# Chunk attention and a two-layer product: values and row sums of a head from one product, and VectorE's weight sums at other steps

## The chip, the cores and the metric

The kernel runs on one core of a Trainium2 chip. The metric is the device time of one execution in microseconds (us). The kernel before was run 13 times: the median is 294.53 us, the runs lie between 293.27 and 295.85 us. One execution is also recorded by the hardware profiler; all profile lines come from that execution.

## What is computed

Attention within chunks of 64 tokens, and then two matrix products with a leaky ReLU between them. The inputs q, k and v have 8 batches, 8 heads, 576 tokens and 64 dimensions per head, in float32; `w_in` is 512x2048 and `w_out` is 2048x512.

```python
# per batch, head and chunk of 64 tokens:
scores = q_c @ k_c.T / 8
attn = exp(scores - max);  attn /= attn.sum(-1) + 1e-09
x = (attn @ v_c)  ->  [4608 tokens, 512]
h = x @ w_in
g = maximum(0.01 * h, h)
out = g @ w_out
```

## The kernel before

**Blocks.** The 4608 tokens are worked on in 9 blocks (`j`) of 512 tokens, that is 8 chunks. A block has four head pairs (`kk`); the two heads of a pair lie on partitions 0 to 63 and 64 to 127. The products of block `j` run together with the attention of block `j+1`.

**Attention** of a block and head pair has four parts, called at the steps that the lists `steps` give:

- `attn_t` (t) transposes q and k (on TensorE for the first three blocks, by DMA from block 3 on) and copies the two heads of k into `kd`, a matrix that is zero where the heads would mix. For the very first block one of the two copies is on ScalarE, otherwise both are on VectorE.
- `attn_s` (s) makes the scores of both heads with eight products of 64 columns, and ScalarE takes the exponential into `e`.
- `attn_x` (x) makes the row sums `zp` with one product of 512 columns against `onesd` (ones within a head, zero across), and the values `xp` with eight products of 64 columns against `VD`. `VD` holds v for one head and zeros, set once by `clear_vd`, for the other. ScalarE then takes `Ln` of the sums and `Exp` of its negative: the reciprocals `rz`.
- `attn_n` (n) multiplies `xp` by `rz` on VectorE into `xT`, the input of the first product.

**Products.** In step n = 0 to 15 of a block, `mm1` makes one 128-row slice of h from four products of 512 columns, and ScalarE turns it into `gT` with the leaky ReLU. In steps 16 to 31, block 0 makes the second product plainly (`mm2`, four parts of w_out by four slices of tokens). Blocks 1 to 8 make it with seven products instead of eight (M1 to M7, after Strassen), in two halves `u` of seven steps each: `mm2s`, 14 steps of eight products of 256 columns. It needs sums of quarters of w_out (`w_sums`, and `w_in_place`, which overwrites two quarters) and sums of quarters of g (`g_sums`), all on VectorE. ScalarE copies M3 and M4 out of PSUM, and VectorE combines the rest.

**Order and buffers.** The order on each engine is the order in which the program is written (`manual_schedule`): nothing reorders it, and each engine takes its instructions one after the other. Within a step the product comes first, then the attention parts of that step in the order n, x, s, t, then the sums and casts. PSUM has eight banks: four for attention (tag "at") and four for the products ("mm"). A tile takes the bank that has been free longest, and a product that writes a bank waits for the reader of the tile that was there. `rz` has two buffers. SP issues loads and stores, GpSimd the loads that change the type; GpSimd also casts keys and, for the first blocks, queries.

Of the kernel before, what the change touches and what calls it, by code (L numbers as in the profile page):

```python
# [9 lines left out]
FP32 = mybir.dt.float32  # L10
ALU = mybir.AluOpType
AFT = mybir.ActivationFunctionType
# [3 lines left out]
def kernel(  # L16
# [9 lines left out]
    nc = tc.nc  # L26
# [5 lines left out]
    CH = 64  # L32
    NKK = H // 2
    NFC = d_ff // 128
    TB = 512
    NJ = n_tok // TB
    NC = TB // CH
    R = 4
    NI = CH // R
    NPT = 3  # L40
# [10 lines left out]
    onesd = sb.tile([128, 128], FP16, name="onesd")  # L51
# [9 lines left out]
    NVD = 2  # L61
    KD = [sb.tile([128, NC, 2, CH], FP16, name=f"kd{m}") for m in range(NKD)]
    VD = [sb.tile([128, NKK, NC, 2, CH], FP16, name=f"vd{m}") for m in range(NVD)]
# [1 line left out]
        nc.vector.memset(t[0:64, :, 1, :], 0.0)  # L65
        nc.vector.memset(t[64:128, :, 0, :], 0.0)

    def clear_vd(m, eng):
        eng.memset(VD[m][0:64, :, :, 1, :], 0.0)
        eng.memset(VD[m][64:128, :, :, 0, :], 0.0)  # L70

    clear_vd(0, nc.vector)

    w_in = sb.tile([128, NKK, d_ff], FP16, name="w_in")
    w_out = sb.tile([128, NFC, d_model], FP16, name="w_out")
# [20 lines left out]
    def sbuf(shape, dtype, name, bufs):  # L96
        return sb.tile(shape, dtype, name=name, tag=name, bufs=bufs)

    def psum(shape, dtype, name, tag):
        return ps.tile(shape, dtype, name=name, tag=tag, bufs=4)  # L100
# [74 lines left out]

    def attn_t(j, kk):

        if j < NPT:  # L180
            tp = psum([128, 2, R, 128], FP16, "tp", "at")
            tk = psum([128, 2, R, 128], FP16, "tk", "mm") if j == 0 else tp
            for a, t in enumerate((tp, tk)):
                for r in range(R):
                    nc.tensor.transpose(
                        out=t[:, a, r, :], in_=half[j][a][:, kk, r, :, :], identity=ident
                    )
            qt = sbuf([128, R, 128], FP16, "qt", 2)
            nc.vector.tensor_copy(out=qt, in_=tp[:, 0, :, :])
            kt = tk[:, 1, :, :]  # L190
        else:
            qt, kt = (t[:, kk, :, :] for t in trans[j])
        kd = KD[(j * NKK + kk) % NKD]
        for hh in range(2):
            p0 = hh * 64
            dst = kd[p0:p0 + 64, :, hh, :].rearrange("p c (i r) -> p c i r", r=R)
            src = kt[p0:p0 + 64, :, :].rearrange("p r (c i) -> p c i r", i=NI)
            if j == 0 and kk < 3 and hh == 0:
                nc.scalar.activation(out=dst, in_=src, func=AFT.Copy, bias=0.0, scale=1.0)
            else:  # L200
                nc.vector.tensor_copy(out=dst, in_=src)  # L201
        live[j, kk] = (qt, kd)
# [16 lines left out]

    def attn_x(j, kk):  # L220

        e = live[j, kk]
        zp = psum([128, TB], FP32, "zp", "at")
        nc.tensor.matmul(out=zp, lhsT=onesd, rhs=e, start=True, stop=True)  # L224
        xp = psum([128, R, 128], FP32, "xp", "at")
        for c in range(NC):
            nc.tensor.matmul(  # L227
                out=xp[:, :, c * NI:(c + 1) * NI],
                lhsT=VD[j % NVD][:, kk, c, :, :],
                rhs=e[:, :, c * NI:(c + 1) * NI],  # L230
                start=True,
                stop=True,
            )
        rz = sbuf([128, TB], FP32, "rz", 2)
        nc.scalar.activation(out=rz, in_=zp, func=AFT.Ln, bias=0.0, scale=1.0)  # L235
        nc.scalar.activation(out=rz, in_=rz, func=AFT.Exp, bias=0.0, scale=-1.0)  # L236
        live[j, kk] = (xp, rz)

    def attn_n(j, kk):

        if j not in xT:
            xT[j] = sbuf([128, NKK, TB], FP16, "xT", 2)
        xp, rz = live.pop((j, kk))
        nc.vector.tensor_tensor(  # L244
            out=xT[j][:, kk, :], in0=xp.rearrange("p r t -> p (r t)"), in1=rz, op=ALU.mult
        )

    STEPS = (attn_t, attn_s, attn_x, attn_n)

# [43 lines left out]
    wv = w_out.rearrange("p (i e) (h m) -> p e h i m", e=2, h=2)  # L293
    ws = {n: sb.tile([128, NH, MH], FP16, name=f"ws_{n}") for n in ("b11_22", "b11_12", "b21_11")}
    gs: dict[str, bass.AP] = {}

    def tt(eng, out, in0, in1, op):
        eng.tensor_tensor(out=out, in0=in0, in1=in1, op=op)  # L298

    def w_sums(g, eng):  # L300

        i = slice(2 * g, 2 * g + 2)
        b11, b12, b21, b22 = (wv[:, e, h, i, :] for e in range(2) for h in range(2))
        tt(eng, ws["b11_22"][:, i, :], b11, b22, ALU.add)
        tt(eng, ws["b11_12"][:, i, :], b11, b12, ALU.add)
        tt(eng, ws["b21_11"][:, i, :], b21, b11, ALU.subtract)

    def w_in_place(g, eng):

        i = slice(2 * g, 2 * g + 2)  # L310
        tt(eng, wv[:, 0, 1, i, :], wv[:, 0, 1, i, :], wv[:, 1, 1, i, :], ALU.subtract)
        tt(eng, wv[:, 1, 0, i, :], wv[:, 1, 0, i, :], wv[:, 1, 1, i, :], ALU.add)

    def g_quarters(j):
        gv = gT[j].rearrange("p (i e) (h t) -> p h e i t", e=2, h=2)
        return [gv[:, h, e, :, :] for h in range(2) for e in range(2)]

    def g_sums(j, g):

        if g == 0:  # L320
            for n in ("a11_12", "a21_22", "a11_22"):
                gs[n] = sbuf([128, NH, TB // 2], FP16, n, 1)
        i = slice(2 * g, 2 * g + 2)
        a11, a12, a21, a22 = (x[:, i, :] for x in g_quarters(j))
        tt(nc.vector, gs["a11_12"][:, i, :], a11, a12, ALU.add)
        tt(nc.vector, gs["a21_22"][:, i, :], a21, a22, ALU.add)
        tt(nc.vector, gs["a11_22"][:, i, :], a11, a22, ALU.add)
        tt(nc.vector, a21, a21, a11, ALU.subtract)
        tt(nc.vector, a12, a12, a22, ALU.subtract)
# [13 lines left out]
            out=out[j * TB:(j + 1) * TB, :].rearrange("(p r) m -> r p m", r=R)[ti], in_=osb  # L343
        )

    part: dict[str, bass.AP] = {}

    def mm2s(j, u, step):

        a11, a21_11, a12_22, a22 = (g_quarters(j)[n] for n in (0, 2, 1, 3))  # L350
        b11, b12_22, b21_22, b22 = wv[:, 0, 0], wv[:, 0, 1], wv[:, 1, 0], wv[:, 1, 1]
        lo, hi = slice(0, MH), slice(MH, d_model)

        def bank(n):
            part[n] = psum([128, d_model], FP32, "mp", "mm")[:, lo]
# [51 lines left out]
    with tc.manual_schedule():  # L407
# [9 lines left out]
        for step in range(NKK + 2):  # L417
# [10 lines left out]
            p = step - 2  # L428
            if 0 <= p < NKK:
                attn_x(0, p)  # L430
            p = step - 1
# [4 lines left out]
            p = step - 2  # L436
# [7 lines left out]
                mm1_part(0, hp, fc, kk)  # L444
        for fc, hp in enumerate(hps):
            mm1_end(0, hp, fc)
        clear_vd(1, nc.vector)
        alloc(1)
        for kk in range(NKK):
            first = load_qk(1, 2 * kk, 2 * kk + 2)[0]  # L450
# [15 lines left out]

        def regular(first, gap, lags=(0, 3, 5, 7)):
            return [[first + gap * kk + lag for kk in range(NKK)] for lag in lags]

        for j in range(NJ):
# [16 lines left out]
            for n in range(2 * NFC + (16 if j == 0 else 0)):  # L489
                if n >= 2 * NFC:  # L490
                    pass
                elif n >= NFC:
                    if j == 0:
                        mm2(j, *reversed(divmod(n - NFC, 4)))
                    elif n - NFC < 14:
                        mm2s(j, *divmod(n - NFC, 7))
                elif j or n >= len(hps):
                    mm1(j, n)
                if hw_at.get(n, NJ) < NJ:
# [7 lines left out]
                        load_qk(qk_at[n], H // 2, H)  # L507
                        after(first, last, "the first two blocks' operands come first")
                for stage, kk in at.get(n, ()):
                    stage(j + 1, kk)  # L510
                if j and n in (4, 8, 12, 16):
                    g_sums(j, n // 4 - 1)
                if j == 0 and n in (20, 23, 26, 32):
                    w_sums((n - 20) // 3 if n < 32 else 3, nc.vector)
                if j == 1 and n < 4:
                    w_in_place(n, nc.vector)
                if j + 2 < NJ:
                    if n in range(cast_at, cast_at + 8, 2):
                        kk = (n - cast_at) // 2
# [41 lines left out]
```

The softmax here doesn't subtract the row's maximum and nothing guards it: scores larger than these inputs give would overflow.

## Time and profile before

| | us |
|---|---|
| median of 13 runs | 294.53 |
| time of the profiled execution | 294.56 |
| its span, first to last instruction | 292.8 |
| TensorE busy (matmul) | 278.0, 95% |
| VectorE busy | 210.3, 72% |
| ScalarE busy | 159.9, 55% |
| GpSimd busy | 107.4, 37% |

The time is 1.76 us more than the span. The share of an engine is an average over stages: the first block has short waits of all engines on each other, and from block 3 on one engine works without a gap. A start-to-start distance between two instructions of one engine is shorter than the duration that the record of one shows[...].

### The profile page before, as it was taken

Reading aid. Unit: us, or ns where it says so; the run is one execution under the profiler, and the core shown is the slowest. Engines: PE = TensorE matmul, PEld = TensorE weight load, DVE = VectorE, ACT = ScalarE, POOL = GpSimd, SP = SyncE. Lnnn points to the kernel's source line nnn. Section 1 sums busy time; section 2 is a strip of 40 time slices with the busy share of each in tenths; the row PEclk is TensorE's granted clock in tenths of the full one; section 3 lists DMA queues with packets and bytes.
Section 4 is the critical chain, followed back from the end, with each engine's and each line's share of the span. In section 5 each row is a group of like instructions: output and inputs, shape, how many; then the busy total and the mean of one; then the engine's idle time right before and its main releaser. Section 6 shows DMA issues by size and latency. Waiting matters only on the chain.

```text
span 292.8 us, 5954 instructions
## 1 busy us (share of the span) xinstructions
PE 278.0 (95%) x2264; PEld 179.3 (61%) x2264; DVE 210.3 (72%) x462; ACT 159.9 (55%) x288; POOL 107.4 (37%) x165
## 2 busy tenths in 40 slices
PE   6979997999799989999999999999999999999994
PEld 2544544446674468557854785488448844884583
DVE  6371455999974898799789779787778748863554
ACT  2567514467245755586358636853684378436610
POOL 5673755844950391087078009406400000000000
PEclk9999999999999999999999999999999999999999
DMA  8999999999999999999978996996770120021011
GB/s 182 232 161 240 244 200 218 238 227 194 194 121 219 273 111 222 185 224 203 238 198 108 231 195 164 170 304 128 110 143 2 73 75 0 2 92 55 0 72 74
DMA packets 92605, 46.28 MB, mean 158 GB/s; under 512 B 65440, under 2 KB 87968, under 8 KB 92576
## 3 DMA queue, kind: packets, MB, share of 16 engines
q1 hardware_dynamic: 68896, 39.33, 58.6%
q0 software_dynamic: 23680, 6.56, 21.5%
q8 instruction: 18, 0.29, 0.4%
q14 instruction: 11, 0.09, 0.1%
HBM read 36.70 MB, written 9.44 MB: 158 GB/s over the span
## 4 chain that ended last, share of the span: by engine, by line
PE 67%; DVE 3%; issue 0%; ACT 0%
PE mp L333 31%; PE hp L251 31%; PE sp L209 2%; PE xp L227 2%; PE zp L224 2%; DVE kd L201 1%; DVE a L298 1%; DVE qh L156 1%; DVE gT L298 0%; ACT gT L262 0%; DVE osb L298 0%
## 5 line engine op out<-in xcount | busy, mean ns | idle before, releaser
L251 PE MATMUL hp<-xT,w_in 128*128 128x512 f16 x576 | 130.9, 379 | 0.2 <-DVE xT L244 0.2
L262 ACT ACTIVATE gT<-hp 128x512 f16<-128x512 f32 x144 | 84.9, 596 | 48.2 <-PE hp L251 47.8
L251 PEld LDWEIGHTS <-w_in 128*128 128x128 f16 x576 | 54.3, 98 | 60.1 <-DMA w_in<-in_moe_w_in_dram 0.8
L298 DVE TENSOR_TENSOR a<-gT 128x512 f16<-128x512 f16 x96 | 40.1, 472 | 24.8 <-ACT gT L262 24.3
L333 PEld LDWEIGHTS <-gT 128*128 128x128 f16 x512 | 49.8, 98 | 7.4
L156 POOL CAST kh<-kf 128x512 f16<-128x512 f32 x36 | 24.8, 704 | 79.9 <-DMA kf<-in_k_dram 75.1
L137 POOL DMA_DIRECT2D vd<-in_v_dram x64 | 43.5, 697 | 2.5 <-DMA w_out<-in_moe_w_out_dram 2.1
L298 DVE TENSOR_TENSOR osb<-mp,m 128x256 f32<-128x256 f32 x64 | 26.9, 422 | 16.1 <-ACT e L217 8.4
L333 PEld LDWEIGHTS <-a 128*128 128x128 f16 x384 | 35.8, 98 | 3.8
L235 ACT ACTIVATE rz<-zp 128x512 f32<-128x512 f32 x36 | 21.4, 595 | 29.0 <-PE zp L224 27.8
L333 PE MATMUL mp<-ws_b,gT 128*128 128x256 f16 x256 | 33.2, 273 | 0.0
L333 PE MATMUL mp<-w_out,gT 128*128 128x256 f16 x256 | 32.0, 273 | 0.0
L201 DVE COPY kd<-kT 64x512 f16<-64x512 f16 x48 | 30.7, 639 | 0.3
L333 PE MATMUL mp<-w_out,a 128*128 128x256 f16 x256 | 30.9, 273 | 0.0
L244 DVE TENSOR_TENSOR xT<-xp,rz 128x512 f16<-128x512 f32 x36 | 24.6, 685 | 7.2 <-ACT rz L236 5.6
L165 POOL CAST vd<-vf 64x512 f16<-64x512 f32 x36 | 24.6, 684 | 10.0 <-DMA vf<-in_v_dram 8.0
L217 ACT ACTIVATE e<-sp 128x512 f16<-128x512 f32 x36 | 21.3, 592 | 11.3 <-PE sp L209 11.2
L298 DVE TENSOR_TENSOR gT<-gT 128x512 f16<-128x512 f16 x64 | 26.9, 461 | 0.0
L236 ACT ACTIVATE rz<-rz 128x512 f32<-128x512 f32 x36 | 22.7, 630 | 1.1
L209 PEld LDWEIGHTS <-kd 128*128 128x128 f16 x288 | 12.7, 100 | 11.3 <-DVE kd L201 8.3
L227 PEld LDWEIGHTS <-vd 128*128 128x128 f16 x288 | 13.6, 99 | 7.8 <-issue 1.5
L367 ACT ACTIVATE m<-mp 128x256 f32<-128x256 f32 x16 | 6.1, 383 | 21.3 <-PE mp L333 21.3
(44 smaller groups left out, 212.1 us busy)
## 6 DMA issues: line engine op xcount, KB each, us to landing
out_dram<-osb SPq DMA_DIRECT2D x36, 256.0 KB, 3.0
w_in<-in_moe_w_in_dram POOLq DMA_DIRECT2D x4, 512.0 KB, 7.6
w_out<-in_moe_w_out_dram POOLq DMA_DIRECT2D x4, 512.0 KB, 13.0
qf<-in_q_dram SPq DMA_DIRECT2D x4, 384.0 KB, 7.8
kf<-in_k_dram SPq DMA_DIRECT2D x4, 384.0 KB, 11.6
qf<-in_q_dram SPq DMA_DIRECT2D x5, 256.0 KB, 6.7
kf<-in_k_dram SPq DMA_DIRECT2D x5, 256.0 KB, 7.2
qf<-in_q_dram SPq DMA_DIRECT2D x2, 640.0 KB, 9.5
```

The lines of the kernel that those rows point to most:

```text
L137: eng.dma_start(out=dst, in_=v[b, h, s:s + n, :].rearrange("(c p) d -> p c d", p=CH))
L156: eng.tensor_copy(out=half[j][a][:, kk, :, :, :], in_=raw[j][a][:, 2 * kk:2 * kk + 2, :].rearrange("p h (r d) -> p r h d", r=R),)
L165: nc.gpsimd.tensor_copy(out=dst, in_=src)
L201: nc.vector.tensor_copy(out=dst, in_=src)
L217: nc.scalar.activation(out=e, in_=sp, func=AFT.Exp, bias=0.0, scale=SCL)
L235: nc.scalar.activation(out=rz, in_=zp, func=AFT.Ln, bias=0.0, scale=1.0)
L236: nc.scalar.activation(out=rz, in_=rz, func=AFT.Exp, bias=0.0, scale=-1.0)
L244: nc.vector.tensor_tensor(out=xT[j][:, kk, :], in0=xp.rearrange("p r t -> p (r t)"), in1=rz, op=ALU.mult)
L251: nc.tensor.matmul(out=hp, lhsT=w_in[:, kk, fc * 128:(fc + 1) * 128], rhs=xT[j][:, kk, :], start=(kk == 0), stop=(kk == NKK - 1),)
L262: nc.scalar.activation(out=gT[j][:, fc, :], in_=hp, func=AFT.Prelu, bias=0.0, scale=1.0, alpha=0.01)
L298: eng.tensor_tensor(out=out, in0=in0, in1=in1, op=op)
L333: nc.tensor.matmul(out=o, lhsT=a[:, i, u * 128:(u + 1) * 128], rhs=b[:, i, :], start=(i == 0), stop=(i == NH - 1),)
```

## The change

Five things are changed together.

1. `VD` holds ones, not zeros, beside v (`ones_vd` in place of `clear_vd`). In `attn_x` the product against `onesd` is gone. Instead of eight products over all 128 rows there are 16 over 64 rows each, one for each head and chunk, alternating between the two row halves and between two banks `xa` and `xb`. A bank has the values of one head on its own 64 partitions and that head's row sums on the other 64.
2. `Ln` is therefore two instructions (each from the other half's partitions), and `attn_n` two multiplications, each over 64 partitions and 512 columns.
3. In `attn_t` from block 3 on, when it is called at step 16 or later, ScalarE makes one of the two key copies.
4. `mm2s` goes through its 14 steps in another order: M3 and M4 of both halves first.
5. `w_sums` and `w_in_place` are called at other steps of block 0 (`w_in_place` was in block 1), and `g_sums` takes its first four slices at once at step 8 for blocks above 2, where it was two and two at steps 4 and 8.

```diff
-    def clear_vd(m, eng):
-        eng.memset(VD[m][0:64, :, :, 1, :], 0.0)
-        eng.memset(VD[m][64:128, :, :, 0, :], 0.0)
+    def ones_vd(m, eng):
+        eng.memset(VD[m][0:64, :, :, 1, :], 1.0)
+        eng.memset(VD[m][64:128, :, :, 0, :], 1.0)
...
-            if j == 0 and kk < 3 and hh == 0:
+            if hh == 0 and (j == 0 and kk < 3 or j >= NPT and n >= NFC):
                 nc.scalar.activation(out=dst, in_=src, func=AFT.Copy, bias=0.0, scale=1.0)
...
         e = live[j, kk]
-        zp = psum([128, TB], FP32, "zp", "at")
-        nc.tensor.matmul(out=zp, lhsT=onesd, rhs=e, start=True, stop=True)
-        xp = psum([128, R, 128], FP32, "xp", "at")
+        xs = [psum([128, R, 128], FP32, n, "at") for n in ("xa", "xb")]
         for c in range(NC):
-            nc.tensor.matmul(
-                out=xp[:, :, c * NI:(c + 1) * NI],
-                lhsT=VD[j % NVD][:, kk, c, :, :],
-                rhs=e[:, :, c * NI:(c + 1) * NI],
-                start=True,
-                stop=True,
-            )
+            for hh, x in enumerate(xs):
+                rows = slice(hh * CH, (hh + 1) * CH)
+                nc.tensor.matmul(
+                    out=x[:, :, c * NI:(c + 1) * NI],
+                    lhsT=VD[j % NVD][rows, kk, c, :, :],
+                    rhs=e[rows, :, c * NI:(c + 1) * NI],
+                    start=True,
+                    stop=True,
+                )
         rz = sbuf([128, TB], FP32, "rz", 2)
-        nc.scalar.activation(out=rz, in_=zp, func=AFT.Ln, bias=0.0, scale=1.0)
+        for hh, x in enumerate(xs):
+            nc.scalar.activation(
+                out=rz[hh * CH:(hh + 1) * CH, :],
+                in_=x[(1 - hh) * CH:(2 - hh) * CH, :, :].rearrange("p r t -> p (r t)"),
+                func=AFT.Ln, bias=0.0, scale=1.0,
+            )
...
-        nc.vector.tensor_tensor(
-            out=xT[j][:, kk, :], in0=xp.rearrange("p r t -> p (r t)"), in1=rz, op=ALU.mult
-        )
+        for hh, x in enumerate(xs):
+            rows = slice(hh * CH, (hh + 1) * CH)
+            nc.vector.tensor_tensor(
+                out=xT[j][rows, kk, :],
+                in0=x[rows, :, :].rearrange("p r t -> p (r t)"),
+                in1=rz[rows, :],
+                op=ALU.mult,
+            )
...
+    ORDER = [(0, 0), (0, 1), (1, 0), (1, 1)] + [(u, s) for u in range(2) for s in range(2, 7)]
...
+        W_SUMS, W_IN_PLACE = (20, 24, 27, 30), (21, 25, 32, 33)
...
-                        mm2s(j, *divmod(n - NFC, 7))
+                        mm2s(j, *ORDER[n - NFC])
...
-                if j and n in (4, 8, 12, 16):
-                    g_sums(j, n // 4 - 1)
-                if j == 0 and n in (20, 23, 26, 32):
-                    w_sums((n - 20) // 3 if n < 32 else 3, nc.vector)
-                if j == 1 and n < 4:
-                    w_in_place(n, nc.vector)
+                sums_at = {8: (0, 4)} if j > 2 else {4: (0, 2), 8: (2, 4)}
+                sums_at |= {12: (4, 6), 16: (6, 8)}
+                if j and n in sums_at:
+                    g_sums(j, *sums_at[n])
+                if j == 0 and n in W_SUMS:
+                    w_sums(W_SUMS.index(n))
+                if j == 0 and n in W_IN_PLACE:
+                    w_in_place(W_IN_PLACE.index(n))
```

## The prediction, made before the changed kernel ran

> **What bounds the kernel now.** I read the page's busy shares, the waits of TensorE, the chain that ended last, stretches of one block each, the groups by line, and the timelines of VectorE and ScalarE at three places. First the busy shares and TensorE's waits (us in total, times, longest):
>
> ```profile
> PE 278.0 (95%) x2264; PEld 179.3 (61%) x2264; DVE 210.3 (72%) x462; ACT 159.9 (55%) x288; POOL 107.4 (37%) x165
> ```
>
> ```profile
> PE sp L209 <- DVE kd L201: 4.7, 6, 1.5
> PE op L277 <- DMA w_out<-in_moe_w_out_dram: 1.8, 1, 1.8
> ```
>
> TensorE is the bound, and waits in few places: for key copies, once for weights. TensorE's timeline places them: in the first attention (15.4, 17.9 us), 1.75 us for w_out at 45.44, then for key copies 0.51 at 65.35, 1.54 at 78.01, 0.61 at 82.54 (block 1), 0.91 at 105.05 (block 2). One later block (us; share of each engine, with counts), and a piece of the chain in it:
>
> ```profile
> 205.17:233.94 28.77, 28.77 (x245) 19.48 (x244) 21.74 (x53) 17.40 (x32) 2.82 (x4) 1.00 0.45 83
> ```
>
> ```profile
> 210.58 0.21 PE zp L224
> 210.80 0.23 PE xp L227 x8
> 211.03 4.32 PE hp L251 x20
> ```
>
> Blocks 3 to 7 take 28.77 us each, with TensorE busy in all of it. So x costs 0.446 us of path per head pair (sums 0.215, values 8 products in 0.23, 29 ns each). What VectorE and ScalarE do costs nothing there while it comes in time. The groups that the change multiplies (busy, mean ns):
>
> ```profile
> L201 DVE COPY kd<-kT 64x512 f16<-64x512 f16 x48 | 30.7, 639 | 0.3
> L235 ACT ACTIVATE rz<-zp 128x512 f32<-128x512 f32 x36 | 21.4, 595 | 29.0 <-PE zp L224 27.8
> L244 DVE TENSOR_TENSOR xT<-xp,rz 128x512 f16<-128x512 f32 x36 | 24.6, 685 | 7.2 <-ACT rz L236 5.6
> ```
>
> **What the Trainium skill says.** TensorEngine Tiling (Array Packing), Key Properties: tiles of the array work independently, but changing the tiling mode drains TensorE. TensorE: Matmul & The Clock Gate, Part 3 (packing small matmuls): matmuls in different row groups start some 4 ns apart; its Part 1 states a start-to-start floor of about 25 ns. Nothing in the trace has 64 rows, so none of the three is shown; the 29 ns above fit the floor. VectorE: DVE Perf Modes, Zero memsets can be issued as uint32: a memset takes a cycle per element whatever the type, and only zeros get the half count. The trace agrees with the half: `vd` was cleared as 64x1024 uint32.
>
> **The change part by part.** Baseline is the profiled span, 292.8; the time is 1.76 more (294.56 against the median 294.53).
>
> *The products of x.* The columns streamed are the same: 512 + 8x64 before, 16x64 after. From below: the two halves stream together and the switches cost nothing, 8 x (29 + 4) = 0.26 us. From above: no overlap, 16 x 29 = 0.46, and each of two switches shows the whole latency of a matmul, 193 - 27 = 0.166 (a 64-column record less its columns): 0.79. I take overlap (0.26) and two drains of about half that latency (0.17): 0.43, no change against 0.446. Ends: -0.19 and +0.34 per call, about 32 calls not otherwise hidden.
>
> *Ones for zeros, at the start.* VectorE before:
>
> ```profile
> 3.16 0.91 DVE L69 MEMSET vd<- 64x1024 uint32 x1 [0.25 <-issue]
> 4.32 0.91 DVE L70 MEMSET vd<- 64x1024 uint32 x1 [0.25 <-issue]
> 5.26 0.72 DVE L156 CAST qh<-qf 128x512 f16<-128x512 f32 x1
> ```
>
> The cast starts without a wait: the memsets, not the load, hold the first queries. Start to start a memset is 1.16 us for 1024 elements and 0.36 for 256, so 1.04 ns each; 2048 elements take 2.2, two of them +2.1 us. The first attention is a serial chain, and four more doubled pieces join it: pair 0's second multiplication ahead of pair 3's copies 0.6 (start to start), pair 1's, whose bank pair 3's scores take, 0.6, pair 3's second `Ln` 0.5 and multiplication 0.6. Sum +4.4: the third slice of `mm1`, complete at 21.35 before, comes at 25.7. Of this, 1.75 falls into the wait for w_out, which is a transfer and does not move (loads are not behind the memsets in any queue), and 0.32 into two waits for GpSimd at 42. Left: +2.3. The second pair of memsets (21.5) is followed by 6 us of idle VectorE; without that it would be +2.1.
>
> *End of block 0.* Here four x stand at steps 25 to 28, one product apart (1.3 us). ScalarE per pair: 1.2 us before, 1.7 after; VectorE 0.6, then 1.2. Before:
>
> ```profile
> 47.58 0.60 ACT L235 ACTIVATE rz<-zp 128x512 f32<-128x512 f32 x1 [6.10 <-PE zp L224]
> 48.21 0.63 ACT L236 ACTIVATE rz<-rz 128x512 f32<-128x512 f32 x1
> 48.75 0.58 ACT L217 ACTIVATE e<-sp 128x512 f16<-128x512 f32 x1
> ```
>
> I count from the end of pair 0's x (47.61 before). Now both banks of a pair are held until the multiplication, where `zp` was free after `Ln`. In the changed program pair 1's `xb` takes the bank of pair 3's scores: it waits for `e` (behind Ln, Ln, Exp) to 2.25, where TensorE is there at 1.1. Pair 3's banks are pair 1's: they wait for pair 1's multiplications, which stand on VectorE behind the output copy of step 28 (4.9 to 5.5) and end at 6.75; TensorE is there at 4.9. Then pair 3's x to 7.2, its copies, Ln, Ln, Exp to 9.0; VectorE's queue (copy, pair 2, copy, pair 3) ends at 11.85. Block 1's first slice needs that, and got it at 7.8 before (55.38). Cost +4.1 (ends 2.5 and 5).
>
> *Block 1 and 2.* Half of `w_in_place` (1.8 of 3.58 us) now lies in block 0's idle VectorE, and TensorE comes some 6 us later while GpSimd's casts, which slow VectorE here (sums of 1.1 us take 2.4), are bound to loads and stay. The new wait: `w_in_place` at steps 21 and 25 must let TensorE finish reading that part of w_out. Pair 3's key copies (step 22) stand behind the first; part 0 is read at step 19, so nothing is late, and if it were, the price is the 1.75 us that TensorE waits at 45.44 anyway. `w_sums` at 27 and 30 stand behind multiplications that are later still. M3 and M4 first move four of the six combinations behind pair 3's copies (1.5 us earlier), against 0.6 for a second multiplication. I let the waits of 2.66 go but for 0.3: block 1 -2.2 with 0.16 lost at its end (below); block 2 -0.7 of 0.91.
>
> *Blocks 3 to 7.* VectorE in the middle of a block before:
>
> ```profile
> 212.40 0.69 DVE L244 TENSOR_TENSOR xT<-xp,rz 128x512 f16<-128x512 f32 x1 [0.67 <-ACT rz L236]
> 213.00 1.21 DVE L201 COPY kd<-kT 64x512 f16<-64x512 f16 x2
> 214.24 1.09 DVE L298 TENSOR_TENSOR a<-gT 128x512 f16<-128x512 f16 x3
> ```
>
> From the block's start, `rz` of pair 0 comes at 7.7 (second `Ln`). Then in VectorE's order: two multiplications 1.2, two copies 1.2, the merged sums 5 x 0.6 = 3.0, the next five 1.75, two multiplications 1.2, two copies 1.25: 17.35. The third scores want them at 222.09 - 205.17 = 16.92: +0.45, as the sums moved from step 4 (idle before) to 8. The merging itself saves 5 fixed parts of 0.07. At the end of the block ahead, pair 3's multiplication ran from 204.67 to 205.35; the second ends 0.6 later, at 205.95, and TensorE wants it after three products of the new block, at 205.17 + 0.65 = 205.82: +0.15 with the semaphore. Five blocks x 0.6 = +3.0 (ends 0.8, if the middle one has half a us of slack that I missed, and 6 where GpSimd slows VectorE). The key copy on ScalarE (0.59, six times) and the order of the halves cost and bring nothing here: ScalarE is 17.4 of 28.8 busy, the last copy is not late. Without that cover a copy costs 0.6.
>
> Sum: 0 + 2.3 + 4.1 - 2.2 - 0.7 + 3.0 = +6.5. Span 299.3, time 301.1 (2.2% slower).
>
> **Rivals.** *Row halves overlap fully* (place: every x; price: 0.25 us or less). For: the skill's 4 ns. Against: the drain. It takes 32 x 0.19 = 6.1; with the other terms at their low ends (2.3 + 2.5 - 2.66 - 0.9 + 0.8 = +2.0) the span is 288.7, with the middle ones 293.2: 290.5 to 295, I say 292.5, faster. It decides from 0.38 us per call with the low ends, 0.24 with the middle ones. *Dear switches*: x near 0.75 in every call, +0.3 x 32 = 9.6 less about 2 that falls into the waits: 308.7. For: two latencies are the natural size of a drain. Against: the drain may be of the array only. *Hidden anyway*: the doubled work finds slack, blocks 3 to 7 lose 0.8 and block 0's end 2.5, x is unchanged: 292.8 + 2.3 + 2.5 - 2.9 + 0.8, time 297.3. For: VectorE is 76% busy in such a block. Against: the chain above is in series.
>
> **How the numbers follow.** Forecast 0.43 (own range 298 to 304), full overlap 0.23, hidden 0.19, dear switches 0.15. Leaving a tenth on each side, half of the overlap case below and two thirds of the dear one above, gives 292.5 to 306. A measurement can tell about 0.2% (0.6 us) from no change. Faster is most of the overlap case, 0.21; same 0.06, from its upper end and the lower end of the hidden one; slower 0.73.
>
> **What would show it.** The group of x: 16 products from start to the next line in 0.43 us; gaps around it tell the drains. The first `hp` complete near 25.7, and still no gain by 45. TensorE waiting for `e` and `xT` between steps 26 and 28 of block 0, block 1 about 6 us late. Waits for `kd` at 65 and 82 gone, new ones of 0.45 before the third scores and 0.15 at each block's start. Wrong if x is far from 0.43, or if blocks 3 to 7 keep 28.77 less a gain.

## The result, and the profile after

The changed kernel takes 314.93 us (median of 11 runs, 313.83 to 316.93), the kernel before 294.67 in runs beside it: a ratio of 1.0698, 95% interval 1.0673 to 1.0723. It is 7.0% slower; the prediction said slower by 2.2%, and its range ended at 306.0. The profiled execution has a span of 312.1 us, 19.3 more than before.

The busy shares, and then TensorE's waits (us in total, times, longest):

```profile
PE 280.5 (90%) x2516; PEld 173.9 (56%) x2516; DVE 224.3 (72%) x461; ACT 188.3 (60%) x331; POOL 103.5 (33%) x165
```

```profile
PE sp L209 <- DVE kd L201: 8.4, 15, 0.9
PE hp L262 <- DVE xT L252: 5.9, 9, 1.8
PE tp L185 <- DVE qh L156: 3.4, 1, 3.4
PE xa L228 <- ACT e L217: 2.0, 2, 1.5
```

TensorE fell from 95 to 90% busy. It waits for key copies 15 times where it did 6 times, and for the multiplications (`xT`) at the start of all eight blocks. One later block took 28.77 us before; now (us; busy time of each engine, with counts):

```profile
219.31:250.24 30.93, 29.42 (x274) 18.73 (x272) 23.33 (x51) 20.86 (x37) 1.47 (x3) 1.00 0.42 78
```

TensorE's timeline in that block shows where the 2.17 us lie:

```profile
220.41 2.97 PE L262 MATMUL hp<-xT,w_in 128*128 128x512 f16 x13 [0.29 <-DVE xT L252]
...
230.62 0.41 PE L209 MATMUL sp<-qT,kd 128*128 128x64 f16 x8 [0.52 <-DVE kd L201]
...
232.37 0.38 PE L262 MATMUL hp<-xT,w_in 128*128 128x512 f16 x1
232.68 0.20 PE L228 MATMUL xa<-e,vd 64*128 64x64 f16 x1
232.69 0.20 PE L228 MATMUL xb<-e,vd 64*128 64x64 f16 x1
...
232.90 0.19 PE L228 MATMUL xb<-e,vd 64*128 64x64 f16 x1
233.02 2.76 PE L262 MATMUL hp<-xT,w_in 128*128 128x512 f16 x12
...
238.10 0.41 PE L209 MATMUL sp<-qT,kd 128*128 128x64 f16 x8 [0.57 <-DVE kd L201]
...
245.20 0.39 PE L209 MATMUL sp<-qT,kd 128*128 128x64 f16 x8
```

The figure in brackets counts idle time from the modelled end of the product before; measured against an undisturbed block (second scores 10.18, third 16.92 us after its start), four things are late: the start by 0.45, then the second scores by 0.69 more, the third by 0.73, the fourth by 0.30. Together 2.17. The x between them is cheap. Two row halves start 3 or 4 ns apart in the trace's own nanoseconds (0 or 10 in the rounded lines), a pair of them every 29 or 30 ns. The first starts 0.31 us after the product ahead of it, where two such products are 0.22 apart, and the next product starts 0.12 after the last. From the product ahead to the product behind that makes 0.65 us; with the sums and the Values of before it was 0.66.

Set block by block against before, by the first slice of `mm1` that has all four pairs (us by which it comes later than before), the shift is as follows (where that slice doesn't wait, as in most blocks before, it is taken 0.65 us, three products, after the block's start):

| reached | later by | term of the stage | predicted |
|---|---|---|---|
| end of pair 0's x, step 25 of block 0 | 2.6 | start 2.6 | 2.3 |
| block 1's first slice (63.26 against 55.38) | 7.9 | end of block 0: 5.3 | 4.1 |
| block 2's | 7.1 | block 1: -0.8 | -2.2 |
| block 3's | 7.7 | block 2: +0.6 | -0.7 |
| block 8's | 19.1 | blocks 3 to 7: +11.4 | +3.0 |
| end of the span | 19.3 | last block: +0.2 | 0 |

The 11.4 us are five times 2.17 and 0.50 more before the fourth scores of block 4. The ScalarE and VectorE groups that were doubled (busy us, mean ns):

```profile
L252 DVE TENSOR_TENSOR xT<-xa,rz 64x512 f16<-64x512 f32 x36 | 24.4, 679 | 28.4 <-ACT rz L242 28.0
...
L237 ACT ACTIVATE rz<-xa 64x512 f32<-64x512 f32 x36 | 21.4, 595 | 21.9 <-PE xb L228 21.2
L201 DVE COPY kd<-kT 64x512 f16<-64x512 f16 x41 | 25.6, 625 | 0.7
L252 DVE TENSOR_TENSOR xT<-xb,rz 64x512 f16<-64x512 f32 x36 | 25.0, 695 | 0.8
...
L237 ACT ACTIVATE rz<-xb 64x512 f32<-64x512 f32 x36 | 21.2, 589 | 0.9
```

An instruction on 64 partitions takes what one on 128 took (589 to 595 ns against 595 for the `Ln`, 679 to 695 against 685 for the multiplication). And its neighbours overlap with it less: VectorE in the same block,

```profile
227.90 0.68 DVE L252 TENSOR_TENSOR xT<-xa,rz 64x512 f16<-64x512 f32 x1 [4.51 <-ACT rz L242]
228.61 0.69 DVE L252 TENSOR_TENSOR xT<-xb,rz 64x512 f16<-64x512 f32 x1
229.34 1.22 DVE L201 COPY kd<-kT 64x512 f16<-64x512 f16 x2
230.59 1.90 DVE L309 TENSOR_TENSOR a<-gT 128x1024 f16<-128x1024 f16 x3
...
234.61 0.75 DVE L309 TENSOR_TENSOR gT<-gT 128x512 f16<-128x512 f16 x2
235.40 0.68 DVE L252 TENSOR_TENSOR xT<-xa,rz 64x512 f16<-64x512 f32 x1
236.11 0.69 DVE L252 TENSOR_TENSOR xT<-xb,rz 64x512 f16<-64x512 f32 x1
236.84 1.20 DVE L201 COPY kd<-kT 64x512 f16<-64x512 f16 x2
```

shows 0.71 from one multiplication to the next and 0.73 to the copy, where before it was 0.60 from the one multiplication to the copy: 1.44 for what had taken 0.60. On ScalarE the two `Ln` start 0.62 apart. Between 227.90 and 238 VectorE is never idle: each pair's late multiplications push its copies, the sums, the next multiplications and the next copies.

### The profile page after: what moved, and what is told of

It reads as the page before. It is cut to its first block, busy times and chain, and to the rows that moved or that the text cites. A ratio compares the mean times of both kernels' runs of the same rounds, so it can differ in the third digit from the quotient of the medians.

```text
span 312.1 us, 6496 instructions
## 1 busy us (share of the span) xinstructions
PE 280.5 (90%) x2516; PEld 173.9 (56%) x2516; DVE 224.3 (72%) x461; ACT 188.3 (60%) x331; POOL 103.5 (33%) x165
## 4 chain that ended last, share of the span: by engine, by line
PE 51%; DVE 32%; ACT 8%; issue 6%; POOL 1%; DVEq 0%
PE hp L262 21%; PE mp L344 20%; DVE xT L252 10%; DVE kd L201 7%; DVE a L309 5%; ACT rz L237 5%; DVE gT L309 4%; PE op L288 4%; PE sp L209 2%; PE xa L228 2%; ACT rz L242 2%; DVE osb L309 2%; DVE m L309 2%; PE tp L185 1%; ACT kd L199 1%
## 5 line engine op out<-in xcount | busy, mean ns | idle before, releaser
L262 PE MATMUL hp<-xT,w_in 128*128 128x512 f16 x576 | 132.3, 379 | 5.9 <-DVE xT L252 5.9
L273 ACT ACTIVATE gT<-hp 128x512 f16<-128x512 f32 x144 | 83.0, 595 | 46.8 <-PE hp L262 46.7
L156 POOL CAST kh<-kf 128x512 f16<-128x512 f32 x36 | 22.5, 639 | 86.5 <-DMA kf<-in_k_dram 86.2
L252 DVE TENSOR_TENSOR xT<-xa,rz 64x512 f16<-64x512 f32 x36 | 24.4, 679 | 28.4 <-ACT rz L242 28.0
L309 DVE TENSOR_TENSOR a<-gT 128x512 f16<-128x512 f16 (+1 forms) x78 | 34.6, 499 | 13.8 <-ACT gT L273 13.3
L237 ACT ACTIVATE rz<-xa 64x512 f32<-64x512 f32 x36 | 21.4, 595 | 21.9 <-PE xb L228 21.2
L165 POOL CAST vd<-vf 64x512 f16<-64x512 f32 x36 | 23.6, 656 | 19.3 <-DMA vf<-in_v_dram 11.5
L201 DVE COPY kd<-kT 64x512 f16<-64x512 f16 x41 | 25.6, 625 | 0.7
L252 DVE TENSOR_TENSOR xT<-xb,rz 64x512 f16<-64x512 f32 x36 | 25.0, 695 | 0.8
L309 DVE TENSOR_TENSOR gT<-gT 128x512 f16<-128x512 f16 (+1 forms) x52 | 24.8, 518 | 0.0
L237 ACT ACTIVATE rz<-xb 64x512 f32<-64x512 f32 x36 | 21.2, 589 | 0.9
```

The lines of the kernel that those rows point to most:

```text
L156: eng.tensor_copy(out=half[j][a][:, kk, :, :, :], in_=raw[j][a][:, 2 * kk:2 * kk + 2, :].rearrange("p h (r d) -> p r h d", r=R),)
L165: nc.gpsimd.tensor_copy(out=dst, in_=src)
L237: nc.scalar.activation(out=rz[hh * CH:(hh + 1) * CH, :], in_=x[(1 - hh) * CH:(2 - hh) * CH, :, :].rearrange("p r t -> p (r t)"), func=AFT. ...
L252: nc.vector.tensor_tensor(out=xT[j][rows, kk, :], in0=x[rows, :, :].rearrange("p r t -> p (r t)"), in1=rz[rows, :], op=ALU.mult,)
L262: nc.tensor.matmul(out=hp, lhsT=w_in[:, kk, fc * 128:(fc + 1) * 128], rhs=xT[j][:, kk, :], start=(kk == 0), stop=(kk == NKK - 1),)
L273: nc.scalar.activation(out=gT[j][:, fc, :], in_=hp, func=AFT.Prelu, bias=0.0, scale=1.0, alpha=0.01)
```

## The experiments

Theory 1: x costs TensorE what it did; the loss is lateness from the doubled `Ln` and multiplications. Theory 2: the 64-row products or the switches between tile shapes cost. Theory 3: the reorderings (merged sums, order of the halves, a key copy on ScalarE) make the waits. Ratios are to the kernel before, in runs beside it, with 95% intervals.

### The reorderings without [V | 1]

```diff
-        xs = [psum([128, R, 128], FP32, n, "at") for n in ("xa", "xb")]
...
+        zp = psum([128, TB], FP32, "zp", "at")
+        nc.tensor.matmul(out=zp, lhsT=onesd, rhs=e, start=True, stop=True)
+        xp = psum([128, R, 128], FP32, "xp", "at")
...
-        eng.memset(VD[m][0:64, :, :, 1, :], 1.0)
+        eng.memset(VD[m][0:64, :, :, 1, :], 0.0)
...
```

> The reorderings alone: the changed kernel with the old attention core (sums by zp, values by xp, zeros in vd, one Ln and one multiplication a pair). Theory 1 (the loss comes from the doubled 64-row Ln and multiplications, late on ScalarE and VectorE): blocks 3 to 7 go back to 28.77 us, the end of block 0 to 7.8 us after pair 0's x, and the waits of 2.66 us in blocks 1 and 2 shrink: 292 to 294 us. Theory 2 (the 64-row products or their switches cost): the same here, 292 to 294. Theory 3 (the merged sums, the order of the halves and the key copy on ScalarE make the waits of blocks 3 to 7): those blocks stay near 30.9, 304 to 306 us.

Measured: 293.59 us, ratio 0.9953 (0.9920 to 0.9986), span 290.7. Blocks 1, 2, 3 and a later one:

```profile
53.54:85.75 32.21, 30.89 (x277) 21.18 (x276) 29.91 (x61) 17.50 (x32) 20.90 (x31) 1.00 1.12 196
85.75:115.36 29.61, 28.95 (x247) 19.41 (x244) 22.56 (x51) 19.65 (x34) 12.10 (x18) 1.00 1.07 211
115.36:145.39 30.03, 28.95 (x247) 19.38 (x244) 22.70 (x47) 18.48 (x33) 13.33 (x18) 1.00 1.19 215
202.93:231.70 28.77, 28.77 (x247) 19.46 (x245) 20.50 (x47) 18.38 (x33) 1.58 (x3) 1.00 0.52 83
```

Theory 3 is out as the cause of the loss. Blocks 1 and 2 gain 1.88 and 0.61 (they took 34.09 and 30.22), so the gain predicted for them (2.2 and 0.7) exists where [V | 1] doesn't use it up. Block 3 loses 1.26: TensorE waits 1.08 us for keys there, with merged sums ahead of them.

### [V | 1] without the reorderings

```diff
-        zp = psum([128, TB], FP32, "zp", "at")
...
+        xs = [psum([128, R, 128], FP32, n, "at") for n in ("xa", "xb")]
...
```

> [V | 1] alone, on the kernel before: its own order of products, its own sums, both key copies on VectorE. Theory 1: the start costs 2.6, the end of block 0 5.3; in blocks 3 to 7 the wait at the start (0.45) and before the second scores (0.69) stay, that before the third scores goes as the sums are not merged behind the multiplications, that before the fourth shrinks to between 0 and 0.3: 5.7 to 7.2 over five blocks; sum 308 to 311 us. Theory 2: all of the loss is here, 314 to 316. Theory 3: the start alone, 296 to 298.

Measured: 318.88 us, ratio 1.0852 (1.0791 to 1.0913), more than any of the three forecasts: the whole loss is here, and the reorderings take 4 us of it back. A later block takes 31.1 to 31.6, with waits before the second, third and fourth scores (0.50, 0.48, 0.44 in brackets). That contradicts a detail of theory 1 as I had put it: the wait before the third scores doesn't come from merging the sums, since it is there without.

### One Ln and one multiplication, with all 16 products

```diff
-        for hh, x in enumerate(xs):
-            nc.scalar.activation(
-                out=rz[hh * CH:(hh + 1) * CH, :],
-                in_=x[(1 - hh) * CH:(2 - hh) * CH, :, :].rearrange("p r t -> p (r t)"),
-                func=AFT.Ln, bias=0.0, scale=1.0,
-            )
+        nc.scalar.activation(
+            out=rz, in_=xs[1].rearrange("p r t -> p (r t)"), func=AFT.Ln, bias=1.0, scale=0.0
+        )
...
+            out=xT[j][:, kk, :], in0=xs[0].rearrange("p r t -> p (r t)"), in1=rz, op=ALU.mult
...
```

> The changed kernel with its 16 row-half products, but one Ln and one multiplication of 128 partitions a pair, in place of two of 64 each. Left out: the normalisation (the Ln is of a constant, and Values of the second head and its sums are mixed up). Theory 1: the loss goes but for the start (0.5 to 2.6) and a little at the end of block 0, where both banks of a pair are still held until the multiplication: blocks 3 to 7 back to 28.8, 294 to 297 us. Theory 2: the products are all there, so the loss is too: 312 to 315. Theory 3: blocks 3 to 7 stay near 30.9, 305 to 308.

Measured: 294.27 us, ratio 1.0007 (0.9972 to 1.0041). A later block:

```profile
205.22:233.98 28.76, 28.76 (x274) 19.00 (x272) 20.43 (x47) 18.44 (x33) 1.47 (x3) 1.00 0.45 83
```

The stretch has 274 products, as in the changed kernel, and takes 28.76 us, where before it was 28.77. From block 1's first whole slice to block 3's it is 61.3 us, as with the reorderings alone (61.5), against 63.8 in the changed kernel; from the end of pair 0's x in block 0 to block 1's first whole slice it is 7.8 us, as before. Theory 2 is out: 16 row-half products with their switches cost TensorE what one product for the sums and eight for the Values cost. One remark on the expectation: here the bank of `xb` is free after the `Ln`, since the multiplication reads only `xa`; so of the end of block 0 this run shows less than it said.

### One of the two doubled instructions at a time

The chain theory: a pair's x, two `Ln`, `Exp`, two multiplications, two key copies, next scores must fit into five products' time; the next three runs take pieces out of it. First one `Ln` (the first half of the edit above), with two multiplications:

> The changed kernel with one Ln of 128 partitions and still two multiplications a pair. Left out: the normalisation (the Ln is of a constant). Chain theory: rz comes 0.62 earlier; of a later block's waits 0.69 becomes 0.07, 0.73 becomes 0.11, 0.30 goes, and the 0.45 at the start, where the multiplications follow an output combination and not rz, stays: 5 x 1.54 less, and about 2 at the start and the end of block 0: 305 us. Rival (half of the loss belongs to each doubled instruction, in proportion): 304 to 305 here and in the next run alike.

Measured: 309.78 us, ratio 1.0501 (1.0453 to 1.0549). Then two `Ln` and one multiplication (the second half of that edit):

> The changed kernel with two Ln and one multiplication of 128 partitions a pair. Left out: the second head's Values in xT are replaced by sums. Chain theory: 0.71 less in VectorE's part of the chain: all four waits of a later block shrink to 0.04 or nothing, 5 x 2.1 less, and about 3 at the end of block 0, 1 at the start: 300 us. Rival (in proportion): 304 to 305.

Measured: 296.97 us, ratio 1.0068 (1.0044 to 1.0091). A later block takes 30.20 us with one `Ln`, 28.76 with one multiplication. Neither the chain's figures (305 and 300 us) nor equal shares (304 to 305 in both) were right: one `Ln` brings 0.73 of 2.17 a block, one multiplication all of it. VectorE with one `Ln` shows why:

```profile
224.73 0.68 DVE L249 TENSOR_TENSOR xT<-xa,rz 64x512 f16<-64x512 f32 x1 [3.76 <-ACT rz L239]
...
231.46 0.76 DVE L306 TENSOR_TENSOR gT<-gT 128x512 f16<-128x512 f16 x2
232.25 0.68 DVE L249 TENSOR_TENSOR xT<-xa,rz 64x512 f16<-64x512 f32 x1
232.96 0.69 DVE L249 TENSOR_TENSOR xT<-xb,rz 64x512 f16<-64x512 f32 x1
233.69 1.21 DVE L201 COPY kd<-kT 64x512 f16<-64x512 f16 x2
```

Its multiplications at 232.25 come straight after the sums. `rz` is there early, and VectorE's queue makes the third scores late (by 0.69; with two `Ln` it was 0.73). So the wait before the second scores belongs to the chain through ScalarE and VectorE and goes with either mend; the one before the third belongs to VectorE's queue and goes only with the multiplication. With one multiplication the copies for the third scores end at 223.92, 16.67 us after the block's start, 0.25 before TensorE wants them; with one of each, at 15.94. The slack before the change was about 1 us, one more `Ln` uses up most of it, and whatever comes on top is paid in full.

### Key copies ahead of the multiplications

```diff
-                for s in (3, 2, 1, 0):
+                for s in (0, 3, 2, 1) if j > 2 else (3, 2, 1, 0):
```

> The changed kernel; in blocks 3 to 7 the key copies of a pair stand ahead of the two multiplications of the pair before, instead of behind them (only the order within a step changes). Theory 1, now sharper (the loss of a later block is the length of one chain: x, Ln, Ln, Exp, two multiplications, two copies, next scores, which has five products' time): the copies leave the chain, the waits before the second, third and fourth scores (0.69, 0.73, 0.30) go, that at the block's start (0.45) stays: 5 x 1.72 less, 306 to 307 us. Rival (VectorE has too much work in all, so the waits come back at the sums or the outputs): less than 3 us gained, 312 to 315.

Measured: 306.73 us, ratio 1.0405 (1.0363 to 1.0447); a later block:

```profile
215.29:244.62 29.33, 29.04 (x275) 18.95 (x273) 23.20 (x51) 20.64 (x37) 1.48 (x3) 1.00 0.44 82
```

The same instructions, in another order on VectorE, and 1.6 us of the 2.17 are gone; 0.56 is left, nearly all of it at the block's start. VectorE is not short of time, 23.2 of 29.3 us; what hurt was that copies which need nothing from a pair stood behind that pair's multiplications.

### The start: ones, and the clock

```diff
-        eng.memset(VD[m][0:64, :, :, 1, :], 1.0)
+        eng.memset(VD[m].bitcast(FP32)[0:64, :, :, 1, :], 0.007826805114746094)
...
```

> The changed kernel, its ones written two at a time as 32-bit words, so that each memset has 1024 elements as the zeros before. Theory 1: a memset takes 1.16 us again, the first cast comes 2.1 us earlier, and as the changed program waits for w_out no more, of this between 0.5 and 2.1 us arrives at the end: 312.8 to 314.4. Against it: the start is absorbed by the wait for w_out, which comes back: 314.9.

Measured: 312.81 us, ratio 1.0657 (1.0580 to 1.0735). This interval holds the changed kernel's 1.0698, so the time alone doesn't tell. The span is 0.7 less, though the first transpose came 2.5 us earlier (5.75 against 8.26).

Nothing in the prediction spoke of TensorE's granted clock. The first stretches of the changed kernel (the third figure from the end is the clock) and, last, the first of the kernel before:

```profile
0.00:10.00 10.00, 5.09 (x19) 2.17 (x19) 6.45 (x13) 1.87 (x2) 5.91 (x14) 0.89 1.04 219
10.00:20.00 10.00, 7.09 (x95) 4.09 (x95) 5.91 (x10) 6.27 (x11) 8.65 (x14) 0.84 1.14 186
20.00:30.00 10.00, 6.82 (x65) 3.64 (x65) 6.64 (x9) 6.78 (x12) 3.11 (x5) 0.92 1.18 239
...
0.00:10.00 10.00, 6.90 (x31) 3.02 (x32) 5.32 (x13) 2.47 (x3) 5.27 (x13) 1.00 1.01 208
```

In stretches of 2 us the changed kernel's clock was 0.50 from 8 to 10 and 0.53 from 18 to 20. But the 1.00 of the kernel before is not what its products show. Three idle products of 512 columns, twice in the kernel before (L394) and twice in the changed one (L407):

```profile
6.88 1.49 PE L394 MATMUL warm<-wz,onesd 128*128 128x512 f16 x3
13.56 0.81 PE L394 MATMUL warm<-wz,onesd 128*128 128x512 f16 x3
...
9.09 1.49 PE L407 MATMUL warm<-wz,onesd 128*128 128x512 f16 x3
11.65 0.81 PE L407 MATMUL warm<-wz,onesd 128*128 128x512 f16 x3
```

They take 1.49 us where the changed kernel's clock was 0.50, and 1.49 us in the kernel before as well, until 13.2 us. So both attentions ran about 7 us at half speed: before from 6.1 to 13.2, in the changed kernel twice 3.4. With the reorderings alone, whose first attention is the same as before, the products ran at full speed from 5.8 us on, and `mm1` began 1.7 us earlier (17.73 against 19.41).

The Trainium skill, TensorE: Matmul & The Clock Gate, Part 1, says that the clock is halved after an idle window of about 3.4 us and that the windows run freely. The changed kernel's first fall fits that: TensorE stood still for 3.42 us before 8.26. The second doesn't: from 14 to 18 TensorE was busy for 1.64 of 4 us. So:

```diff
-        keep_warm(8)
+        keep_warm(14)
...
-            if step < NKK:
-                keep_warm(3)
+            keep_warm((3, 3, 6, 6, 6, 0)[step])
```

> The changed kernel with more idle products on TensorE in its first attention (14 instead of 8 ahead, 6 instead of 3 in the later steps), so that the granted clock, which fell to 0.50 at 8 to 11 and 18 to 21 us, stays at 1.00. Theory: transposes, scores and x at half clock lengthen the serial chain of the first attention by 0.5 to 1.5 us: 313.4 to 314.4 us. Against it: the chain there is ScalarE's and VectorE's, and the clock costs nothing: 314.9.

Measured: 313.16 us, ratio 1.0633 (1.0572 to 1.0694), a little less than forecast; this interval, too, overlaps the changed kernel's. From 5 to 30 us the clock is 1.00, and block 0's first output product starts at 38.30 instead of 39.76. Of these 1.46 us 0.38 are there already at the first transposes (7.88 against 8.26), which wait for a cast on VectorE; the other 1.1 go with the clock. At block 1's first slice 0.5 is left in the profile (62.79 against 63.26). The clock fell at the end of block 0 in this execution (0.83 between 50 and 60); whether that took the rest was not tried.

The larger memsets are not on the path for 2.1 us. The second pair's transposes start at 8.80 with the faster ones, at 9.41 with the faster ones and the idle products together (the last run below), and at 10.15 with the idle products alone. So 0.7 to 1.4 of 2.1 us are left there, since GpSimd casts that pair's queries behind a load (TensorE waits 0.61 and 1.01 for it). In the last run the clock fell to 0.50 between 10 and 13 us, and block 0's first output product came at 38.63, no earlier than 38.30.

### x of block 0 spread out

```diff
-                0: [[10, 14, 18, 22], [13, 17, 21, 25], [25, 26, 27, 28], [27, 28, 29, 30]],
+                0: [[10, 14, 18, 22], [13, 17, 21, 25], [18, 22, 26, 28], [20, 24, 28, 30]],
```

> The changed kernel; the four x of block 0 stand at steps 18, 22, 26 and 28 instead of 25 to 28, their multiplications two steps behind. Theory (the end of block 0 lost 5.3 us since four doubled chains and held banks fall into four steps): block 1's first slice comes 3.5 to 5 us earlier, and most of it stays: 310 to 312 us. Rival (VectorE's total work at the end of block 0 is what counts, or the two late waits move into block 1): 314 to 315.

Measured: 311.47 us, ratio 1.0548 (1.0495 to 1.0601). Block 1's first whole slice starts at 59.23 instead of 63.26: 4.0 of the 5.3 us are the crowding of four doubled chains into four steps. In the changed kernel the waits there are

```profile
52.69 0.19 PE L228 MATMUL xb<-e,vd 64*128 64x64 f16 x1 [1.10 <-ACT e L217]
...
56.73 0.19 PE L228 MATMUL xa<-e,vd 64*128 64x64 f16 x1 [1.37 <-DVE xT L252]
...
63.26 6.42 PE L262 MATMUL hp<-xT,w_in 128*128 128x512 f16 x29 [1.77 <-DVE xT L252]
```

for the banks that the prediction named, and for the last multiplication; the first two are gone when spread.

### All mends together, and a faster kernel without [V | 1]

The last three: the reorderings alone with sums merged only from block 4 on (`if j > 3`); the same with the key copies of block 2, and of the third pair in block 1, a step earlier,

```diff
-                1: [[7, 11, 17, 20], [10, 14, 20, 23], [14, 18, 23, 26], [16, 20, 25, 28]],
-                2: regular(9, 4),
+                1: [[7, 11, 16, 20], [10, 14, 20, 23], [14, 18, 23, 26], [16, 20, 25, 28]],
+                2: [[8, 12, 16, 20]] + regular(9, 4)[1:],
```

and the changed kernel with the mends of all runs but this last one (its key copies of blocks 1 and 2 stay where they were), and the last multiplications of a later block at step 27 instead of 28.

> The reorderings alone, and the sums of steps 4 and 8 merged only from block 4 on (block 3 keeps the two pieces, as its GpSimd is still busy). Theory: the 1.08 us that TensorE waited in block 3 for keys, behind merged sums of 5.0 us, goes; block 3 takes 28.8 instead of 30.03: 292.4 us. Against it: the wait is GpSimd's doing and stays with two pieces: 293.6.

Measured: 292.36 us, ratio 0.9917 (0.9892 to 0.9942). The median is the one forecast, but by luck. The mechanism did half: block 3 takes 29.50 instead of 30.03, its wait for keys is 0.55 instead of 1.08. The profiled span is longer than with the reorderings alone (291.7 against 290.7), and the two intervals overlap.

> The kernel of the run before, and in blocks 1 and 2 the key copies of a pair one step earlier, ahead of the sums of that step. Theory: the waits for keys of 1.12 us in block 1 and 0.66 in block 2 go: 290.6 to 291.5 us. Against it: VectorE is full there and the sums become late instead: 292.4.

Measured: 291.94 us, ratio 0.9893 (0.9854 to 0.9931), a little above the forecast. Block 2 and block 4:

```profile
86.28:115.05 28.77, 28.77 (x247) 19.47 (x245) 22.52 (x51) 19.40 (x34) 13.10 (x19) 1.00 1.01 208
144.67:173.44 28.77, 28.77 (x246) 19.46 (x244) 20.95 (x47) 18.39 (x33) 11.47 (x19) 1.00 1.09 210
```

Block 2 now runs without a wait; block 1 keeps one of 0.88, block 3 one of 0.68. This is the fastest of all kernels here, by 1.1% against before; against the run ahead of it the intervals overlap.

> The changed kernel with all that mends it: ones as 32-bit words, more idle products at the start, x of block 0 spread, sums merged from block 4 on, key copies ahead of multiplications in blocks 3 to 7, and the last multiplications of such a block one step earlier. Theory (what [V | 1] costs is lateness only, and x costs TensorE what sums and Values cost before): start +0.5, end of block 0 +1.5, block starts 5 x 0.15, blocks 1 to 3 like the reorderings alone: 294 to 297 us, and not under the reorderings alone. Rival (the products cost by themselves): over 300.

Measured: 300.11 us, ratio 1.0168 (1.0125 to 1.0210). That is 3 us above the theory's range and just inside the rival's. The rival's reason doesn't hold all the same: later blocks take 29.05 with all their row-half products. But the start and the end of block 0 cost 3.7 us against the reorderings alone (block 1's first whole slice at 59.09 against 55.43), not 2.0, and from there to block 3's first whole slice it takes 64.7 against 62.1, where I had expected no difference. There VectorE has little slack to give: 29.9 of 32.2 us busy in block 1 of the reorderings alone. With these mends [V | 1] is still 1.7% slower than the kernel before. What the earlier key copies in blocks 1 and 2 would bring here was not run.

## Why the prediction was wrong in size

The direction was right and the three rivals fall; the sum failed in its terms. Of the 12.8 us that were missing 8.4 lie in blocks 3 to 7, 2.7 in blocks 1 and 2, 1.2 at the end of block 0 and 0.5 in the rest.

**x of a head pair (0.43 us, no change).** Right, and shown: 28.76 us a block with all 16 products. Both rivals that rested on this term, full overlap with a gain and dear switches with a larger loss, fall; the latter's 308.7 us lies nearest to the measured time, but for a reason that isn't there. The 4 ns that the Trainium skill gives for row groups (TensorE: Matmul & The Clock Gate, Part 3) agrees with the 3 or 4 ns measured. The parts were near too: 0.10 more than between two plain products on the way in, 0.22 from the first row half to the last, 0.12 on the way out, together 0.44.

**Start (+2.3; measured +2.6).** The size is right partly by luck. The doubled chain was there, but longer than forecast: pair 3's last multiplication ends at 26.7 where before it was 21.35, 5.4 later and not 4.4. More of it was taken up, too. The forecast put 1.75 + 0.32 us against it, idle times counted from the modelled end of the product before; from start to start the waits for w_out and for GpSimd at 42 to 45 had cost the kernel before 2.6. Of the terms, the memsets' 2.1 us are in part hidden behind GpSimd's cast of the second pair's queries. The halved clock was not in the sum, but it slowed the profiled execution before for about as long as the changed one, so it doesn't explain the difference between the two.

**End of block 0 (+4.1; measured +5.3).** The mechanism was right: x waits for `e` and then for the multiplications, 4.0 us go when the four x are spread. The term was 1.2 too small, since a `Ln` was counted at 0.5 and a multiplication at 0.6, where they start 0.62 and about 0.72 apart.

**Blocks 1 and 2 (-2.9; measured -0.2).** The gain of the reorderings is real, 2.5 us without [V | 1]. The step that failed is that the waits go "but for 0.3" with [V | 1] too: it set the earlier sums and combinations against one second multiplication of 0.6 and left out that each pair has one, longer than 0.6, and a second `Ln`. New waits take the place of the old ones: for keys at 77.56, 84.82 and 107.85 (0.37, 0.62 and 0.87 in brackets) and for the last multiplication at 96.25 (0.83). With one `Ln` and one multiplication a pair the two blocks take what they take with the reorderings alone (61.3 and 61.5 us, above).

**Blocks 3 to 7 (+3.0; measured +11.4).** Here the forecast failed most: 0.60 us a block was put in, 2.17 was measured. The line that failed is VectorE's order, added up to 17.35 after the block's start (its terms give 17.30). In the changed kernel the same sum, from the starts shown above, is 8.59 + 1.44 + 1.25 + 3.02 + 1.79 + 1.44 + 1.23 = 18.76, and the third scores come at 18.79. So the order was right and its entries were too small. The two pairs of multiplications account for 0.48: their durations were taken from whole-width ones that overlap their neighbours. The rest is nearly all `rz`, which came 8.56 after the start instead of 7.7: the block's start was 0.45 late, which was not carried into this chain, the second `Ln` took 0.62 instead of 0.5, and the first started 0.62 after the leaky ReLU ahead of it, where a whole-width one starts 0.49 after it. Another 0.17 is a slip of reading. TensorE's times in the forecast (205.17 for the block's start, 205.82 for the fourth product) are from the chain view, which puts its instructions later than the timeline, from which VectorE's times were taken. In the timeline the block starts at 205.00:

```profile
205.00 3.62 PE L251 MATMUL hp<-xT,w_in 128*128 128x512 f16 x16
```

The same slip made the wait at the block's start 0.15 where it should have been 0.32; the rest of the measured 0.45 is the second multiplication, which ends 0.70 after the first and not 0.6, and the 0.06 from its end to the product.

The second thing missed is that the chain was followed to one place only, the third scores. The second scores wait too (0.69): there the path is x, two `Ln`, `Exp`, two multiplications, two copies. Each wait moves TensorE and x with it, so they add up and don't overlap: 0.45 + 0.69 + 0.73 + 0.30.

That the key copy on ScalarE and the order of the halves "cost and bring nothing" was wrong as well. With them the fourth wait is 0.30, without them, in the run with [V | 1] alone, about 0.6. The order puts four output combinations ahead of the multiplications of pair 2, which start at 243.15 though `rz` was there at 242.57; the copy on ScalarE spares VectorE one of the two copies. It took 1.09 us instead of 0.59, and seven times instead of six, but ended 1.5 us ahead of VectorE's copy (243.56 against 245.06), so its length cost nothing here. How much of the gain belongs to which was not tried apart. Blaming the merged sums for the third wait was wrong too: with the sums in two pieces it is 0.65 against 0.73.

**The rival that everything hides (297.3)** fell too: the later blocks had about 1 us of slack in the chain that counts, less than one doubled pair uses.

## What to carry to other kernels

Halving the partitions of an elementwise instruction didn't shorten it here (679 to 695 ns against 685); splitting one into two of 64 partitions doubles its engine's part, and where the result is on a serial chain the full double is paid as soon as the slack, here 1 us a pair, is used up. Follow each chain to every consumer in the period, not only to the one that was late last, and add up the waits, since each delays the start of the next chain. Before splitting the work, look for instructions that stand behind it in an in-order queue without needing it: moving the key copies ahead gave back three quarters of the loss in a later block. And when two times are subtracted, take both from the same view, and compare a clock that a view gives with the durations of the products.

## What the runs showed of the hardware that was not expected

- Neighbours on one engine overlap less when the second begins on other partitions than the first. On VectorE multiplications of the two halves start 0.69 to 0.72 us apart. The copy of the first half's keys starts 0.73 after the second multiplication (10 times), but the copy of the second half's keys, on the same 64 partitions as that multiplication, 0.61 or 0.62 after it (5 times):

```profile
243.15 0.68 DVE L252 TENSOR_TENSOR xT<-xa,rz 64x512 f16<-64x512 f32 x1
243.84 0.69 DVE L252 TENSOR_TENSOR xT<-xb,rz 64x512 f16<-64x512 f32 x1
244.46 0.60 DVE L201 COPY kd<-kT 64x512 f16<-64x512 f16 x1
```

With one multiplication of 128 partitions it is the other way round: 0.61 for the first half's copy (10 times), 0.70 to 0.72 for the second half's alone (5 times). So what goes with the lost 0.1 us is the change of the first partition and not the width. ScalarE shows the same: the `Ln` of the first bank, which reads the upper 64 partitions, starts 0.62 after the leaky ReLU ahead of it (12 times), a whole-width `Ln` 0.49 or 0.50 after it (12 times before). The traces don't show why.
- Entering and leaving the 64-row products cost about 0.1 us each (0.31 instead of 0.22, and 0.12 instead of 0.03).
- Ones written as 32-bit words were set as fast as zeros, where the forecast had said that only zeros get the half count: 0.91 us for 64x1024 words, against 1.76 for the same ones in fp16.
- A later block with 28 more products (four times 16 row-half ones for 9 whole ones) takes 28.76 us against 28.77.
- Every profiled execution begins with TensorE at half speed, and it ended anywhere from 4.5 to 13.9 us; the clock in the profile is 1.00 there, and only the durations of the products show it (1.49 us for three of 512 columns against 0.81).
- The clock fell to one half again, for 3.4 to 10.2 us at a time, in the first attention of the changed kernel and of most of its variants, though no wait there was over 3.42 us; with the faster memsets it was at 0.69 from 20 to 30 us, on the first slices of `mm1`. It happened once, for 3.4 us, in the fastest kernel too.
- A ScalarE copy of 64x512 from SBUF to SBUF took 1.09 us (7 of them, 1.08 to 1.11), the one from PSUM 0.59.
